# An attention and two mixtures of experts: a written order for engines through expert 0's second unit to expert 6

## The chip, the cores and the metric

One NeuronCore of a Trainium2 chip runs the whole kernel. The metric is the device time of one execution in microseconds (us), the median of several runs. Engines are named as in the profile: PE (matrix product; PEld is its weight load), DVE (vector), ACT (scalar), POOL (GpSimd), and SP, whose queue issues most DMAs.

## What is computed

Three stages follow each other, each on the output of the one before. N = 1536 tokens, width D = 512, E = 8 experts, inner width F = 1024.

```python
x = chunked_attention(q, k, v, mem_k, mem_v)      # reshaped to (1536, 512)

logits = x @ w_gate                               # first mixture: dense
P = exp(logits - logits.max())
for _ in range(8):                                # the gates are balanced
    P /= P.sum(1) + 1e-9
    P /= P.sum(0) + 1e-9; P *= N / E
out = sum(P[:, e] * (relu(x @ w1[e]) @ w2[e]) for e in range(8))

e_i = argmax(out @ w_gate2)                       # second mixture: top 1
y_i = softmax_weight_i * (relu(out_i @ w1b[e_i]) @ w2b[e_i])
```

All arithmetic is to fp32 accuracy. Each fp32 matrix is held as two fp32r parts, high and low, and each product is made of three: high by high, high by low, low by high.

## The kernel before, in words

**First mixture, direct units.** Expert 0 is done in two units (halves of F, `u` = 0 and 1). A unit takes the tokens in groups; for each group `m1_h` (L393) makes four tiles of the hidden layer, and `m1_y` (L409) one output tile per 128 tokens. In unit 1 the groups have 512 tokens, so 3 groups of 4 + 4 tiles: 24 tiles, each of 12 matmuls with 512 columns. After an `m1_h` tile ACT makes the high part of the hidden layer with a ReLU (L405), and DVE the low part (L406); after an `m1_y` tile DVE adds PSUM into `acc` (L423). There are two PSUM buffers for either kind of tile (tags `ph` and `py`).

**Experts 1 to 6** use a Strassen-like scheme with seven products in place of eight (`m1_g`, L464). For each quarter `fi` of the inner width and each half `n` of the tokens, `m1_g` makes seven products of 6 matmuls with 384 columns into four PSUM tiles A, B, C, D, and forms four hidden blocks from sums of them in the SBUF scratch `stmp` (`s1`, `s5`, `w`, `c21`). `put` (L488) lets ACT make the ReLU (L492) and DVE the low part (L493) of each block. `m1_d` (L517) then makes six output tiles of 6 matmuls with 512 columns; each is added into `acc` by DVE (L530). These six tiles lag one step: `flush_d` (L903) issues, after the products of a step, the output tiles of the step before. Output tiles use the tags `ph` and `py` in turn, so a tile can start when the fourth tile before it has been taken out of PSUM.

**What the sums need.** The scheme works on sums of blocks of x. `xs_build` (L430) makes them while unit 1 runs: `three` has POOL form three sums with eight additions and subtractions of 384 columns in `stmp`, ACT make their high part (L449) and DVE the low part (L450) in `tsum`; `one` overwrites a part of `xhi` and `xlo` that had been saved to `xkeep` in DRAM. The weights need sums too: `conv_pair` (L151) takes two raw chunks, and makes seven high and low pairs, ACT the high part (L157), POOL the low one (L158) and four sums between them (L164 to L170). Other chunks are converted one at a time by `chunk_conv` (L131; L145 on ACT, L146 on POOL). After a conversion `chunk_dma` (L119) issues the next load on SP's queue; there are four raw buffers.

**Gates.** `sinkhorn_start` and eight `sinkhorn_iter` (L359, L372) balance the gates; each iteration has four DVE operations on rows, one small matmul with a matrix of ones (`cs`), and five DVE operations on columns. `scale_expert0` (L387) then multiplies the 12 tiles of `acc` by their gates on ACT.

**What sets the order.** Outside of the last stage the order on each engine is chosen by the framework's scheduler: it takes what is written as a priority and fills engines with what it believes to be ready. What it has chosen is fixed in the program: each engine runs its own queue strictly in that order, and an instruction whose input is late holds up all that stand behind it. Within `tc.manual_schedule()` (used before for the jobs of the second mixture) the instructions keep the written order.

Of the kernel before, what the change touches and what calls it, by code (L numbers as in the profile page):

```python
# [9 lines left out]
F32 = mybir.dt.float32  # L10
# [10 lines left out]
P = 128  # L21
# [11 lines left out]
def kernel(  # L33
# [97 lines left out]
    def chunk_conv(eng=None, defer=False):  # L131
# [3 lines left out]
        if kind == "s":  # L135
            rest = conv_pair(e, u)
            if defer:
                return rest
            rest()
            return  # L140
# [10 lines left out]
    def conv_pair(e, fi):  # L151
# [9 lines left out]
        split("a11", a11)  # L161
        split("a12", a12)
        split("a22", a22)
        nc.gpsimd.tensor_tensor(a22, a21, a22, ALU.add)  # L164
        split("s1", a22)
        nc.gpsimd.tensor_tensor(a21, a11, a21, ALU.subtract)
        nc.gpsimd.tensor_tensor(a11, a22, a11, ALU.subtract)
        split("s2", a11)
        split("s3", a21)
        nc.gpsimd.tensor_tensor(a12, a12, a11, ALU.subtract)  # L170

        def rest():
            split("s4", a12)
            done[0] += 2
            chunk_dma(2)

        return rest
# [181 lines left out]
    def sinkhorn_start():  # L359
        m = smallp.tile([P, 1], F32, tag="gm", name="gm")  # L360
        nc.vector.tensor_reduce(out=m, in_=lsb, axis=AX.XY, op=ALU.max)
        mt = ps_a.tile([P, P], F32, tag="pa", name="mt")
        nc.tensor.transpose(mt[0:1, :], m, ident)
        m1 = smallp.tile([1, 1], F32, tag="m1", name="m1")
        nc.vector.tensor_reduce(out=m1, in_=mt[0:1, :], axis=AX.X, op=ALU.max)
        mb = ps_a.tile([P, 1], F32, tag="pa", name="mb")
        nc.tensor.matmul(mb, ones[0:1, :], m1, start=True, stop=True)
        nm = smallp.tile([P, 1], F32, tag="nm", name="nm")
        nc.vector.tensor_scalar_mul(nm, mb, -1.0)
        nc.scalar.activation(pr, lsb, AF.Exp, bias=nm)  # L370

    def sinkhorn_iter():  # L372
        rs = smallp.tile([P, NT, 1], F32, tag="rs", name="rs")
        nc.vector.tensor_reduce(out=rs, in_=pr, axis=AX.X, op=ALU.add)
        nc.vector.tensor_scalar_add(rs, rs, EPS)
        nc.vector.reciprocal(rs, rs)
        nc.vector.tensor_tensor(pr, pr, rs.to_broadcast([P, NT, E]), ALU.mult)
        cs = ps_a.tile([P, NT, E], F32, tag="pa", name="cs")
        nc.tensor.matmul(cs.rearrange("p t e -> p (t e)"), ones, pr.rearrange("p t e -> p (t e)"), start=True, stop=True)
        ct = smallp.tile([P, 1, E], F32, tag="ct", name="ct")  # L380
        nc.vector.tensor_reduce(out=ct.rearrange("p a e -> p e a"), in_=cs.rearrange("p t e -> p e t"), axis=AX.X, op=ALU.add)
        nc.vector.tensor_scalar_add(ct, ct, EPS)
        nc.vector.reciprocal(ct, ct)
        nc.vector.tensor_scalar_mul(ct, ct, float(N) / E)
        nc.vector.tensor_tensor(pr, pr, ct.to_broadcast([P, NT, E]), ALU.mult)
# [44 lines left out]
    def xs_build():  # L430

        steps = []
# [6 lines left out]
        def three(kk, n):  # L439
# [8 lines left out]
            for i, x in ((0, x22), (1, x12), (2, x21)):  # L448
                nc.scalar.copy(tsum[:, i, 0, kk, c], x)  # L449
                nc.vector.tensor_tensor(tsum[:, i, 1, kk, c], x, f32(tsum[:, i, 0, kk, c]), ALU.subtract)  # L450
# [13 lines left out]
    def m1_g(e, fi, n):  # L464
# [23 lines left out]
        def put(key, x):  # L488
# [658 lines left out]
```

## Time and profile before

| | us |
|---|---|
| median of 3 runs (1366.89 to 1368.7) | 1367.07 |
| the profiled execution | 1369.2 |
| span of its trace | 1367.4 |
| PE busy | 1301.5 (95%) |
| DVE busy | 728.5 (53%) |
| POOL busy | 451.2 (33%) |
| ACT busy | 435.2 (32%) |

The span runs from the first to the last traced instruction, and the profiled execution's own time is 1.8 us longer. Busy time of PE is that of modelled, overlapping matmuls, so gaps between them and the granted clock say more than the share. In time the span divides so: attention with unit 0 up to some 177 us, unit 1 to 255, experts 1 to 6 to some 1016, expert 7 and the routing to some 1185, and the second mixture from there.

### The profile page before, as it was taken

The numbers are of one execution on the slowest core, as the hardware profiler recorded it, in microseconds if no ns is written. First come the engines' busy times: TensorE is split into PE (matmuls) and PEld (weight loads), VectorE is DVE, ScalarE is ACT, GpSimd is POOL, SyncE is SP. The second block draws the span as 40 slices with busy tenths as digits, with TensorE's granted clock in tenths as the row PEclk, the third lists the DMA queues.
The fourth block names the chain that finished last, engine by engine and source line by source line (L and its number), as shares of the span: only waits on it lengthen the run. The fifth ranks groups of instructions, "written<-read, shape, count | busy, mean of one in ns | idle before, by whom it ended". The sixth has DMA issues, their size and how long they took to land. (4 is left out here: it accounts for less than half of the span.)

```text
span 1367.4 us, 18950 instructions
## 1 busy us (share of the span) xinstructions
PE 1301.5 (95%) x6892; PEld 1128.5 (83%) x6892; DVE 728.5 (53%) x1429; ACT 435.2 (32%) x927; POOL 451.2 (33%) x557
## 2 busy tenths in 40 slices
PE   8999679999999999999999999999999999989997
PEld 7888558888888888888888888888898888768775
DVE  6666456355555545555555555555653234745566
ACT  4333221523222222232223222222221122444455
POOL 4221870643333333433334444444220012301001
PEclk9999889999999999999999999999999999999999
DMA  9443540111111111111111111111120001476560
GB/s 194 92 93 86 178 164 14 54 32 39 39 32 31 31 31 32 32 31 32 31 31 31 40 38 32 32 31 38 47 93 16 1 8 45 154 235 233 158 204 16
DMA packets 107259, 94.12 MB, mean 69 GB/s; under 512 B 50667, under 2 KB 75243, under 8 KB 107140
## 3 DMA queue, kind: packets, MB, share of 16 engines
q1 hardware_dynamic: 104996, 87.30, 22.0%
q0 software_dynamic: 2000, 5.34, 1.0%
q8 instruction: 58, 0.95, 0.3%
q14 instruction: 61, 0.50, 0.1%
q10 hardware_dynamic: 144, 0.03, 0.0%
HBM read 76.27 MB, written 17.60 MB: 69 GB/s over the span
## 5 line engine op out<-in xcount | busy, mean ns | idle before, releaser
L182 PE MATMUL py<-bh,hbig 128*128 128x512 f32 x960 | 328.0, 394 | 12.4 <-ACT hbig L405 11.9
L182 PE MATMUL ph<-bh,hbig 128*128 128x512 f32 x576 | 204.3, 395 | 21.3 <-DVE acc L530 21.3
L182 PEld LDWEIGHTS py<-bh,hbig 128*128 128x128 f32 x960 | 180.8, 189 | 51.1 <-ACT hbig L405 12.6
L182 PE MATMUL py<-bl,hbig 128*128 128x512 f32 x480 | 188.4, 392 | 0.0
L182 PEld LDWEIGHTS ph<-bh,hbig 128*128 128x128 f32 x576 | 108.1, 188 | 51.3 <-DVE acc L530 30.6
L146 POOL TENSOR_TENSOR bl<-raw,bh 128x512 fp32r<-128x512 f32 x62 | 80.0, 1308 | 201.8 <-ACT bh L145 194.2
L508 POOL TENSOR_TENSOR stmp<-stmp 128x384 f32<-128x384 f32 x48 | 55.8, 1163 | 272.5 <-DVE stmp L506 272.4
L158 POOL TENSOR_TENSOR ws<-raw,ws 128x256 fp32r<-128x256 f32 x168 | 123.0, 746 | 52.0 <-ACT ws L157 50.7
L530 DVE SCALAR_TENSOR_TENSOR acc<-py,pr,acc 128x512 f32<-128x512 f32 x144 | 107.6, 748 | 42.1 <-PE py L182 42.0
L493 DVE SCALAR_TENSOR_TENSOR hbig<-stmp,hbig 128x384 fp32r<-128x384 f32 x144 | 83.0, 619 | 74.7 <-ACT hbig L492 74.7
L486 PE MATMUL sb<-tsum,ws 128*128 128x384 f32 x576 | 117.5, 340 | 0.0
L530 DVE SCALAR_TENSOR_TENSOR acc<-ph,pr,acc 128x512 f32<-128x512 f32 x144 | 107.6, 747 | 17.2 <-PE ph L182 16.4
L486 PE MATMUL sa<-xhi,ws 128*128 128x384 f32 x384 | 114.2, 338 | 0.0
L486 PE MATMUL sc<-xhi,ws 128*128 128x384 f32 x384 | 113.4, 336 | 0.6 <-ACT stmp L501 0.6
L182 PE MATMUL ph<-bl,hbig 128*128 128x512 f32 x288 | 112.9, 392 | 0.0
L493 DVE SCALAR_TENSOR_TENSOR hbig<-sa,hbig 128x384 fp32r<-128x384 f32 x48 | 26.8, 558 | 160.4 <-ACT hbig L492 160.4
L182 PEld LDWEIGHTS py<-bl,hbig 128*128 128x128 f32 x480 | 90.6, 189 | 18.9
L486 PEld LDWEIGHTS sb<-tsum,ws 128*128 128x128 f32 x576 | 103.0, 188 | 0.0
L492 ACT ACTIVATE hbig<-stmp 128x384 fp32r<-128x384 f32 x144 | 67.6, 518 | 97.9 <-POOL stmp L508 97.9
L157 ACT CAST ws<-raw 128x256 fp32r<-128x256 f32 x168 | 65.9, 408 | 90.9 <-POOL raw L164 40.8
L182 PE MATMUL ph<-xhi,ah 128*128 128x512 f32 (+1 forms) x240 | 86.9, 363 | 8.0 <-DVE hbig L406 8.0
L694 DVE TENSOR_TENSOR w<-raw,w 128x512 fp32r<-128x512 f32 x112 | 72.2, 686 | 39.9 <-ACT w L693 39.9
(210 smaller groups left out, 2264.1 us busy)
## 6 DMA issues: line engine op xcount, KB each, us to landing
raw<-in_moe_w_dram SPq DMA_DIRECT2D x176, 256.0 KB
raw<-in_moe_w_dram SPq DMA_DIRECT2D x96, 128.0 KB
disp<-zrow SPq DMA_DIRECT2D x24, 257.0 KB
xg<-disp SPq DMA_DIRECT2D x19, 257.0 KB
vin<-in_v_dram SPq DMA_DIRECT2D x20, 176.0 KB
kin<-in_k_dram SPq DMA_DIRECT2D x12, 256.0 KB
qin<-in_q_dram SPq DMA_DIRECT2D x12, 256.0 KB
out_dram<-zrow SPq DMA_DIRECT2D x12, 256.0 KB
```

The source lines that it names most:

```text
L146: (eng or nc.gpsimd).tensor_tensor(lo, raw, f32(hi), ALU.subtract)
L157: nc.scalar.copy(w[:, 0], x)
L158: nc.gpsimd.tensor_tensor(w[:, 1], x, f32(w[:, 0]), ALU.subtract)
L182: nc.tensor.matmul(ps, l, r, start=(i == 0), stop=(i == n - 1))
L486: nc.tensor.matmul(ps, l, r, start=(i == 0 and not more), stop=(i == len(terms) - 1), skip_group_check=more)
L492: nc.scalar.activation(hh, x, AF.Relu)
L493: nc.vector.scalar_tensor_tensor(hl, x, 0.0, f32(hh), ALU.max, ALU.subtract)
L508: nc.gpsimd.tensor_tensor(s5, w, s5, ALU.add)
L530: nc.vector.scalar_tensor_tensor(a, ps, pr[:, t, e:e + 1], a, ALU.mult, ALU.add)
L694: nc.vector.tensor_tensor(l, raw, f32(h), ALU.subtract)
```

## The change

The scheduler gives way to the written order from unit 1 of expert 0 to the end of expert 6, and the written order itself is new.

- **Unit 1** (`unit_sums`): a table `beside` lists for each of the 24 tiles (called steps 0 to 23 here) what is issued right behind it: the conversion of single chunks at steps 0, 1, 2 and 21; the gate work, cut into three starting parts and eight pairs of a row part and a column part, one part a step from 0 to 18; POOL's part of the four `three` at steps 3, 7, 13, 18, and their ACT and DVE parts (`three_split`) at 6 and 7, 12 and 13, 17 and 18, 22 and 23; the parts of `one` on POOL at 9 and 20, those on DVE and ACT at 12, 13, 22, 23; and the eight parts of the first weight pair at 10 to 12, 14 to 16 and 20. `stmp` grows from four to seven pieces.
- **Experts 1 to 6** (`expert_sums`): the conversion of a weight pair is cut into eight parts (`pair_steps`), two of which are issued at each of two places inside `m1_g`, over both halves of the tokens; the two single chunks are converted behind the second half. In `m1_g` the sum `s5` moves from POOL to DVE, and the low parts of three blocks are issued behind all the sums.
- `scale_expert0` moves from the end of unit 1 into the first quarter of expert 1. The rows of zeros that are written to DRAM (`fills`) are issued one a step; their preparation and the constants of the routing stand at the start of expert 1.

```diff
@@ -158,23 +154,27 @@
-        split("a11", a11)
-        split("a12", a12)
-        split("a22", a22)
-        nc.gpsimd.tensor_tensor(a22, a21, a22, ALU.add)
-        split("s1", a22)
-        nc.gpsimd.tensor_tensor(a21, a11, a21, ALU.subtract)
-        nc.gpsimd.tensor_tensor(a11, a22, a11, ALU.subtract)
-        split("s2", a11)
-        split("s3", a21)
-        nc.gpsimd.tensor_tensor(a12, a12, a11, ALU.subtract)
-
-        def rest():
+        def sums():
+            nc.gpsimd.tensor_tensor(a22, a21, a22, ALU.add)
+            nc.gpsimd.tensor_tensor(a21, a11, a21, ALU.subtract)
+            nc.gpsimd.tensor_tensor(a11, a22, a11, ALU.subtract)
+            nc.gpsimd.tensor_tensor(a12, a12, a11, ALU.subtract)
+
+        def last():
             split("s4", a12)
-            done[0] += 2
             chunk_dma(2)
 
-        return rest
+        done[0] += 2
+        return [
+            lambda: split("a11", a11),
+            lambda: split("a12", a12),
+            lambda: split("a22", a22),
+            sums,
+            lambda: split("s2", a11),
+            lambda: split("s1", a22),
+            lambda: split("s3", a21),
+            last,
+        ]
...
@@ -445,23 +455,28 @@
...
+        def three_split(kk, n, i):
+            c = slice(n * SN, (n + 1) * SN)
+            x = stmp[:, (2, 1, 3)[i], :]
+            nc.scalar.copy(tsum[:, i, 0, kk, c], x)
+            nc.vector.tensor_tensor(tsum[:, i, 1, kk, c], x, f32(tsum[:, i, 0, kk, c]), ALU.subtract)
 
         def one(kk, n):
-            (b11, b12, _, _), _, c2 = parts(kk, n)
-            x11, x12 = stmp[:, 2 * kk, :], stmp[:, 2 * kk + 1, :]
-            nc.gpsimd.tensor_tensor(x11, b11[0], b11[1], ALU.add)
+            (b11, _, _, _), _, _ = parts(kk, n)
+            nc.gpsimd.tensor_tensor(stmp[:, 4 + kk, :], b11[0], b11[1], ALU.add)
...
@@ -490,27 +505,34 @@
...
-            nc.vector.scalar_tensor_tensor(hl, x, 0.0, f32(hh), ALU.max, ALU.subtract)
             hsum[fi, n, key] = (hh, hl)
+            return lambda: nc.vector.scalar_tensor_tensor(hl, x, 0.0, f32(hh), ALU.max, ALU.subtract)
 
         prod(A, "a11")
         nc.scalar.copy(s1, A)
+        for f in first:
+            f()
         prod(B_, "s2")
         nc.vector.tensor_tensor(s1, B_, s1, ALU.add)
         prod(C, "s1")
         nc.scalar.copy(s5, C)
+        for f in second:
+            f()
         prod(D_, "a22")
         prod(A, "a12", True)
-        put((0, 0), A)
+        put((0, 0), A)()
         prod(B_, "s3")
         nc.vector.tensor_tensor(w, B_, s1, ALU.add)
         nc.vector.tensor_tensor(c21, w, D_, ALU.subtract)
-        nc.gpsimd.tensor_tensor(s5, w, s5, ALU.add)
-        put((1, 0), c21)
+        low10 = put((1, 0), c21)
+        nc.vector.tensor_tensor(s5, w, s5, ALU.add)
+        low11 = put((1, 1), s5)
         prod(C, "s4", True)
         nc.vector.tensor_tensor(s1, C, s1, ALU.add)
-        put((0, 1), s1)
-        put((1, 1), s5)
+        low01 = put((0, 1), s1)
+        low10()
+        low11()
+        low01()
...
@@ -907,58 +929,113 @@
...
+        gates = sinkhorn_parts()
+        beside = {i: [] for i in range(24)}
+        for i in range(3):
+            beside[i].append(chunk_conv)
+        for i, f in enumerate(gates):
+            beside[i].append(f)
+        kn = [(kk, n) for n in range(NQ) for kk in range(KH)]
+        for i, a in zip((6, 12, 17, 22), kn):
+            for j in range(3):
+                beside[i + (j > 1)].append(lambda a=a, j=j: three_split(*a, j))
+        for i, a in zip((3, 7, 13, 18), kn):
+            beside[i].append(lambda a=a: three(*a))
+        pair = []
+        beside[9] += [lambda: one(0, 0), lambda: one(1, 0)]
+        beside[12].append(lambda: one_split(0, 0))
+        beside[13].append(lambda: one_split(1, 0))
+        beside[10].append(lambda: pair.extend(pair_steps()))
+        for i in (10, 11, 12):
+            beside[i].append(lambda: pair.pop(0)())
+        beside[12].append(lambda: pair.pop(0)())
+        for i in (14, 15, 16):
+            beside[i].append(lambda: pair.pop(0)())
+        beside[20].append(lambda: pair.pop(0)())
+        beside[20] += [lambda: one(0, 1), lambda: one(1, 1)]
+        beside[21].append(chunk_conv)
+        beside[22].append(lambda: one_split(0, 1))
+        beside[23].append(lambda: one_split(1, 1))
+        it = 0
+        for t0 in range(0, NT, GT)[::-1]:
+            for w in [lambda f=f: m1_h(e, u, t0, GT, f) for f in range(NF)] + [lambda i=i: m1_y(e, u, t0, i) for i in range(GT)]:
+                w()
+                for f in beside[it]:
+                    f()
+                it += 1
+
+    def expert_sums(e):
+        end = e == E - 2
+        for fi in range(NF):
+            plain = end and fi == NF - 1
+            pair = [] if plain else pair_steps()
+            for n in range(NQ):
+                first, second = [], []
+                if plain and n == 0:
+                    first, second = [chunk_conv] * 2, [chunk_conv]
+                elif not plain:
+                    first, second = (pair[:2], pair[2:4]) if n == 0 else (pair[4:6], pair[6:])
+                m1_g(e, fi, n, first, second)
+                if e == 1 and fi == 0:
+                    for t in range(n * SQ, n * SQ + SQ):
+                        scale_expert0(t)
+                        scale_expert0(t + TPB)
+                flush_d()
+                late_d.append((e, fi, n))
+                if n:
+                    conv(1 if plain else 2)
+                if fills:
+                    fills.pop(0)()
...
+                with tc.manual_schedule():
+                    nc.gpsimd.memset(zrow, 0.0)
+                    nc.gpsimd.memset(zrow[:, DM:DM + 1], BIG)
+                    routing_consts()
+                    expert_sums(e)
...
-        if nu == 1:
-            gs = gs[::-1]
-            for i, z in enumerate((xhi, xlo)):
-                nc.sync.dma_start(xkeep[:, i], f32(z[:, 0:KH, S:N]))
-            ast.close()
-            sst = ExitStack()
-            spool = sst.enter_context(tc.tile_pool(name="spool", bufs=1, side="right"))
-            tsum = spool.tile([P, 3, 2, KH, S], F32R, name="tsum")
-            stmp = spool.tile([P, 4, SN], F32, name="stmp")
-            three, one = xs_build()
-            xq = {2: three[0], 5: three[1], 8: three[2], 11: three[3], 14: one[0], 16: one[1], 18: one[2], 20: one[3]}
...
```

The gates' functions are cut at the places named above without other edits (`sinkhorn_parts`).

What the change moves is shown at three places. The first is ACT at the end of unit 0 and the start of unit 1 (`hbig` is the hidden layer, `tsum` the sums of x, `ah` and `bh` chunks of weights, `ws` parts of a pair). Before:

```order
L405 ACTIVATE hbig<-ph 128x256
L449 CAST tsum<-stmp 128x384 x6
L405 ACTIVATE hbig<-ph 128x256 x2
L449 CAST tsum<-stmp 128x384 x3
L405 ACTIVATE hbig<-ph 128x256
L145 CAST ah<-raw 128x512
L405 ACTIVATE hbig<-ph 128x256
L449 CAST tsum<-stmp 128x384 x3
L145 CAST bh<-raw 128x512
```

Now:

```order
L416 ACTIVATE hbig<-ph 128x256
L416 ACTIVATE hbig<-ph 128x512
L139 CAST bh<-raw 128x512
L416 ACTIVATE hbig<-ph 128x512
L139 CAST bh<-raw 128x512
L416 ACTIVATE hbig<-ph 128x512
L139 CAST bh<-raw 128x512
L377 ACTIVATE pr<-lsb,nm 128x96
L416 ACTIVATE hbig<-ph 128x512
L462 CAST tsum<-stmp 128x384 x3
L416 ACTIVATE hbig<-ph 128x512 x3
L153 CAST ws<-raw 128x256
```

Twelve casts of `tsum` stood among the ReLUs of unit 0's last tiles (those of 256 columns), six of them in a row. Now none stands there, and the first three come behind the four ReLUs of unit 1's first group.

The second is POOL in one quarter of an expert (`bl` the low part of a chunk, `raw` the raw buffers). Before:

```order
L508 TENSOR_TENSOR stmp<-stmp 128x384
L146 TENSOR_TENSOR bl<-raw,bh 128x512 x2
L158 TENSOR_TENSOR ws<-raw,ws 128x256 x3
L164 TENSOR_TENSOR raw<-raw 128x2x128
L166 TENSOR_TENSOR raw<-raw 128x2x128
L167 TENSOR_TENSOR raw<-raw 128x2x128
L158 TENSOR_TENSOR ws<-raw,ws 128x256
L170 TENSOR_TENSOR raw<-raw 128x2x128
L158 TENSOR_TENSOR ws<-raw,ws 128x256 x2
L508 TENSOR_TENSOR stmp<-stmp 128x384
L158 TENSOR_TENSOR ws<-raw,ws 128x256
L508 TENSOR_TENSOR stmp<-stmp 128x384
```

Now:

```order
L140 TENSOR_TENSOR bl<-raw,bh 128x512 x2
L154 TENSOR_TENSOR ws<-raw,ws 128x256 x3
L158 TENSOR_TENSOR raw<-raw 128x2x128
L159 TENSOR_TENSOR raw<-raw 128x2x128
L160 TENSOR_TENSOR raw<-raw 128x2x128
L161 TENSOR_TENSOR raw<-raw 128x2x128
L154 TENSOR_TENSOR ws<-raw,ws 128x256 x4
```

The sum `s5` in `stmp` stood once behind a whole pair's sums and once alone; now POOL has no part in the hidden blocks.

The third is DVE at steps 12 and 13 of unit 1, now:

```order
L434 TENSOR_TENSOR acc<-py,acc 128x512
L390 TENSOR_REDUCE ct<-cs 128x8
L391 TENSOR_SCALAR ct<-ct 128x8
L392 RECIPROCAL ct<-ct 128x8
L393 TENSOR_SCALAR ct<-ct 128x8
L394 TENSOR_TENSOR pr<-pr,ct 128x96
L463 TENSOR_TENSOR tsum<-stmp,tsum 128x384 x2
L472 TENSOR_TENSOR stmp<-xhi,xlo 128x384
L473 TENSOR_TENSOR stmp<-stmp 128x384
L475 TENSOR_TENSOR xlo<-stmp,xhi 128x384
L434 TENSOR_TENSOR acc<-py,acc 128x512
```

Between the two additions into `acc` stand a column part, two low parts of sums, and three operations of `one`, which in the order before were spread by the scheduler.

## Rows read from the trace of the kernel before

**Rows 1.** The waits of PE over the span: engine line waited for, us in total, times, longest.

```profile
PE ph L182 <- DVE acc L530: 21.3, 22, 1.5
PE py L182 <- ACT hbig L405: 11.9, 2, 9.8
PE ph L182 <- DVE hbig L406: 8.0, 3, 6.3
```

**Rows 2.** The timeline of PE: start us, us, engine line op out<-in xcount [idle before <-releaser].

```profile
151.21 0.28 PE L182 MATMUL ph<-xlo,ah 128*128 128x256 f32 x1
151.33 0.28 PE L182 MATMUL ph<-xhi,al 128*128 128x256 f32 x1
...
161.44 0.80 PE L182 MATMUL py<-bh,hbig 128*128 128x512 f32 x1 [9.83 <-ACT hbig L405]
...
176.93 0.39 PE L182 MATMUL ph<-xhi,ah 128*128 128x512 f32 x1
...
254.87 0.33 PE L486 MATMUL sa<-xhi,ws 128*128 128x384 f32 x1
```

**Rows 3.** The timeline of ACT in the same stretch.

```profile
158.25 0.51 ACT L449 CAST tsum<-stmp 128x384 fp32r<-128x384 f32 x1 [6.26 <-POOL stmp L445]
```

**Rows 4.** Windows: PE, PEld, DVE, ACT, POOL busy us (xcount); then PEclk, DMA share, GB/s.

```profile
160.00:180.00 20.00, 15.60 (x62) 12.43 (x63) 8.59 (x11) 5.09 (x12) 19.53 (x19) 0.77 0.09 32
220.00:240.00 20.00, 20.00 (x94) 16.61 (x93) 14.24 (x46) 3.34 (x6) 0.00 (x0) 1.00 0.00 1
```

**Rows 5.** The timeline of PE in a slice of expert 2.

```profile
498.10 0.39 PE L182 MATMUL ph<-bh,hbig 128*128 128x512 f32 x1
...
503.35 0.39 PE L182 MATMUL py<-bh,hbig 128*128 128x512 f32 x1
504.68 0.50 PE L182 MATMUL ph<-bh,hbig 128*128 128x512 f32 x1 [0.94 <-DVE acc L530]
```

**Rows 6.** The timelines of POOL, ACT and DVE in that slice; last row the next.

```profile
501.01 1.33 POOL L508 TENSOR_TENSOR stmp<-stmp 128x384 f32<-128x384 f32 x1
...
502.37 0.94 ACT L492 ACTIVATE hbig<-stmp 128x384 fp32r<-128x384 f32 x2 [1.84 <-POOL stmp L508]
...
503.88 0.74 DVE L530 SCALAR_TENSOR_TENSOR acc<-ph,pr,acc 128x512 f32<-128x512 f32 x1
...
517.81 0.75 DVE L530 SCALAR_TENSOR_TENSOR acc<-ph,pr,acc 128x512 f32<-128x512 f32 x1
```

**Rows 7.** The timeline of DVE in the second unit, POOL idle.

```profile
200.68 0.25 DVE L374 TENSOR_REDUCE rs<-pr 128x12 f32<-128x96 f32 x1
201.44 0.26 DVE L377 TENSOR_TENSOR pr<-pr,rs 128x96 f32<-128x96 f32 x1
201.63 0.69 DVE L423 TENSOR_TENSOR acc<-py,acc 128x512 f32<-128x512 f32 x1
...
204.34 0.69 DVE L423 TENSOR_TENSOR acc<-py,acc 128x512 f32<-128x512 f32 x1 [2.03 <-PE py L182]
204.95 0.25 DVE L381 TENSOR_REDUCE ct<-cs 128x8 f32<-128x96 f32 x1
...
205.88 0.26 DVE L385 TENSOR_TENSOR pr<-pr,ct 128x96 f32<-128x96 f32 x1
...
220.57 0.56 DVE L456 TENSOR_TENSOR stmp<-xhi,xlo 128x384 f32<-128x384 f32 x1
```

**Rows 8.** The timeline of DVE in the second unit, POOL at work.

```profile
181.84 2.31 DVE L456 TENSOR_TENSOR stmp<-xhi,xlo 128x384 f32<-128x384 f32 x2
184.07 2.61 DVE L457 TENSOR_TENSOR stmp<-stmp 128x384 f32<-128x384 f32 x2
```

**Rows 9.** The timeline of ACT at the end of the second unit.

```profile
242.54 1.96 ACT L388 ACTIVATE acc<-acc,pr 128x512 f32<-128x512 f32 x3
```

**Rows 10.** The timeline of SP's queue, then a window of 3 us, in expert 3.

```profile
525.93 8.77 SPq L125 DMA_DIRECT2D raw<-in_moe_w_dram  x4
...
539.00:542.00 3.00, 3.00 (x18) 2.79 (x17) 1.44 (x3) 0.48 (x1) 0.00 (x0) 1.00 0.00 0
```

More of the change, by code (lines that the diff above doesn't have):

```diff
@@ L149, in chunk_conv, with pair_steps @@
         chunk_dma()
-    def conv_pair(e, fi):
+    def pair_steps():
+        e, fi = chunks[done[0]][:2]
         r0, r1 = raw_view(raws.pop(done[0])), raw_view(raws.pop(done[0] + 1))
@@ L357 @@
     nc.vector.memset(ones, 1.0)
[L359 to L370, printed above, removed]
@@ L459, in one, with m1_g @@
             nc.vector.tensor_tensor(xlo[:, kk, c2], x12, f32(xhi[:, kk, c2]), ALU.subtract)
-        kn = [(kk, n) for n in range(NQ) for kk in range(KH)]
-        return [lambda a=a: three(*a) for a in kn], [lambda a=a: one(*a) for a in kn]
-    def m1_g(e, fi, n):
+        return three, three_split, one, one_split
+    def m1_g(e, fi, n, first, second):
         c = slice(n * SN, (n + 1) * SN)
@@ L908, in flush_d, with unit_sums @@
                     m1_d(e_, fi_, n_, half, i)
+    def unit_sums(e, u):
+        nonlocal spool, tsum, stmp
+        spool = sst.enter_context(tc.tile_pool(name="spool", bufs=1, side="right"))
+        tsum = spool.tile([P, 3, 2, KH, S], F32R, name="tsum")
+        stmp = spool.tile([P, 7, SN], F32, name="stmp")
+        three, three_split, one, one_split = xs_build()
+        gates = sinkhorn_parts()
[32 more added lines that the diff above has]
+                it += 1
@@ L910 @@
+    spool = tsum = stmp = None
+    sst = ExitStack()
     for nu, (e, u) in enumerate(units):
         last = nu == len(units) - 1
+        if nu == 1:
+            for i, z in enumerate((xhi, xlo)):
+                nc.sync.dma_start(xkeep[:, i], f32(z[:, 0:KH, S:N]))
+            ast.close()
+            with tc.manual_schedule():
+                unit_sums(e, u)
+            psst.close()
+            continue
         if 0 < e < E - 1:
@@ L918 @@
                 zrow = zst.enter_context(tc.tile_pool(name="zp", bufs=1, side="right")).tile([P, ROW], F32, name="zrow")
[L919 to L920 removed]
                 fills = fill_list(zrow)
                 conv(1)
[L923 to L930 removed]
+                with tc.manual_schedule():
+                    nc.gpsimd.memset(zrow, 0.0)
+                    nc.gpsimd.memset(zrow[:, DM:DM + 1], BIG)
+                    routing_consts()
+                    expert_sums(e)
@@ L958 @@
         L = sum(NF + nt for _, nt in gs)
-        convs = ([13, 15, 16, 25] if nu == 0 else [21] if nu == 1 else [4, 7, 10, 14])
-        if nu != 1:
-            convs += [L - 3]
+        convs = ([13, 15, 16, 25] if nu == 0 else [4, 7, 10, 14]) + [L - 3]
         if nu:
@@ L1033 @@
             flush()
-        if nu == 0:
-            post = [sinkhorn_start] + [sinkhorn_iter] * 8
-        if nu == 1:
-            for p_ in post:
-                p_()
-            post = []
-            for t in range(NT):
-                scale_expert0(t)
-            psst.close()
-            routing_consts()
     for f in first_load:
```

105 lines of the change are left out of this document (48 added, 57 removed).

## The prediction

> **What bounds the kernel now.** I read the waits of PE first, since PE has work in nearly every microsecond and nothing else is near full. Over the whole span its three largest waits add up to 41 us [rows 1], and the timelines put all of them between unit 0's end and expert 6, where the change works. They are of two kinds.
>
> *Unit 0's tail and unit 1.* PE's timeline shows the last matmul of a run at 151.33 us, then nothing for 9.83 us; unit 1 starts at 176.93 and expert 1's first product at 254.87 [rows 2]. The reader is to see who ended that pause: a ReLU on ACT. ACT at that time ran a cast of `tsum` at 158.25 after waiting 6.26 us for POOL [rows 3]. The ReLU stood behind that cast in ACT's queue, PE behind the ReLU. In the order before, twelve such casts stand among unit 0's last ReLUs. The windows show the second half of the bill: from 160 to 180 us the granted clock of PE averaged 0.77, between its two levels of 1.2 and 2.4 GHz, and at 220 to 240, after unbroken work, 1.00 [rows 4].
>
> How much is lost there? At 151.4 us unit 0 still had 24 matmuls of 256 columns, at 0.12 us from one to the next [rows 2], and 24 of 512 columns. A tile of 12 of those takes 2.71 us, from one of its two additions into `acc` to the next [rows 7], so 0.226 each. That is 2.9 + 5.4 = 8.3 us. Unit 1 is 24 tiles of 2.71 us, 65.0, and some ten tiny gate matmuls, for which I allow 1.4 together. Needed: 74.7. Taken: 254.87 - 151.45 = 103.4. **28.7 us are lost.**
>
> *Experts 1 to 6.* PE waits 22 times for DVE to take an output tile out of PSUM, 21.3 us [rows 1], with 48 steps in the stage. In one of them the output tiles start at 498.10; the fifth, which needs the first one's buffer, starts at 504.68, 1.33 us after the last matmul before it where 0.23 is normal [rows 5]. So one such wait costs 1.10 us. The chain behind it: POOL makes `s5` at 501.01 behind a whole weight pair's conversion, ACT's ReLU waits 1.84 us for that, DVE's low part waits for the ReLU, and only at 503.88 does DVE take the first tile out, 5.8 us after it was begun [rows 6]. Other steps have no such wait. **22 x 1.10 = 24.2 us.**
>
> **The change part by part.** *1. `s5` on DVE, the pair spread.* POOL leaves the hidden blocks' chain. DVE gains a sum of 384 columns, 0.56 us without POOL beside it [rows 7]. Behind the last product DVE then has at most `s5`, one more sum, three low parts: 5 x 0.56 = 2.8, some 3.1 with the latency. The fifth tile is due 4 x 1.36 = 5.4 us after the first begins, and taking one out lasts 0.74 [rows 6], so DVE may be as late as 4.7. If POOL runs beside all five, each costs 1.16 to 1.31 [rows 8], 6.2 in sum, and 1.5 us of wait come back. I take the low end with one slowed operation, 3.8: a pair's parts are issued behind the first and third of seven products, so POOL is through with them near the last. Term: **-24.2**, bounds -24.2 and +9 (1.5 x 22 in their place).
>
> *2. Casts of `tsum` out of unit 0's ReLUs.* The 28.7 us go, except what is new. POOL keeps the same additions, now beside unit 1; the single chunks' and the pair's conversion move inside unit 1, too. Unit 0's tail keeps its normal change from hidden to output tiles; I leave 1 us for it (0.5 to 2).
>
> *3. DVE in unit 1: the new wait.* The gate's small matmul is issued right behind each tile and waits for the row part of the tile before, and PE's queue stands behind it. At most steps DVE has one addition (0.69) or low part and a row part, 1.02, or column part, 1.19 [rows 7]: under 2.0 of 2.71 us. Steps 12 and 13 are not like that. Step 12 has 0.69 + 1.19, five operations on two SBUF inputs, and a trip to ACT between the last two (0.6); step 13 has 0.69 + 1.02, then four more and a trip. Such an operation lasts 0.56 with POOL idle [rows 7], 1.16 to 1.31 with POOL at work [rows 8].
> With POOL idle: step 12 takes 5.3, step 13's row part ends 0.3 + 5.3 + 1.7 = 7.3 us after the tile of step 12, where PE, two tiles on, wants it after 5.4: 1.9 lost. The rest of step 13 (2.8) and steps 14 and 15 (1.9 + 1.7) end at 13.7, PE wants the next at 4 x 2.71 + 1.9 = 12.7: 1.0 lost. Sum 2.9.
> With POOL at work: step 12 takes 8.5, the row part ends at 10.5, 5.1 lost; then 10.5 + 5.4 + 3.6 = 19.5 against 15.9, 3.6 lost; and steps 22 and 23 with nine such operations run some 4.5 us into expert 1's first step. Sum 13.2. The two longer pauses may also drop the clock to the lower level: the mean of 0.77 over the 20 us that held the pause at 161 and a shorter one is worth 0.23 x 20 = 4.6 us at most [rows 4]. That makes 18.
> At step 12 ACT is itself held by this step's casts, so POOL has little to do; later it is at work. I take 2 + 3.5 for the two waits, 1.5 for the four steps with a low part and a row part in one, 1.5 for the end: **+8.5**, bounds 3 and 18.
>
> Here a rule bears on the sum. The Trainium skill, SBUF — State Buffer, section Who interferes with whom, says that DVE with two SBUF inputs and GpSimd share a port pair as an exclusive lock and that the loser blocks for the whole instruction. The rows agree in kind (0.56 becomes 1.16 to 1.31). By that rule, held throughout, the sum would go to this part's upper bound, which is case (a) below.
>
> *4. Gates on `acc`, 12 multiplications on ACT in expert 1.* Three take 1.96 us [rows 9], six 3.9. They stand behind the first step's ReLUs, and ahead of the second step's copy of product A, which is over 4.2 us (four products of 6 x 0.175) into that step wanted empty; there are no output tiles yet between. The multiplications end some 1.4 + 3.9 us after the first step's products, the copy 0.5 later: **+2** (0 to 4).
>
> *5. Loads and zeros on SP's queue.* The pair's four loads now are issued behind its last part, about 12 us before the next pair's first cast. In the trace four issues went out by 534.7 us, and from 539 no byte moved [rows 10]: 4.3 us at the most. Cover is 12 us, and if it were gone ACT would wait with the ReLUs behind. The zeros go out one a step. 0.
>
> **The sum**: -24.2 - 28.7 + 1 + 8.5 + 2 = -41.4, less than 0.6 either way for the wait in expert 1's first step that is in neither term. Small waits that a fixed order always has somewhere I put at 2: **-39.4**. The profiled execution took 1369.2, so 1329.8; it stands 2.1 above the median of the runs, so **1328 us** in their terms.
>
> **The rivals.**
> (a) *DVE beside POOL is the bound of unit 1*, each of its two-input operations at 1.2 us: +18 and +4 in place of +8.5 and +2, so 1328 + 11.5 = 1340. For it: every such row beside POOL is doubled [rows 7, 8]. Against it: POOL waits for DVE and ACT in turn. Chance 0.15. The page of the Trainium skill on SBUF named above would have it so.
> (b) *DVE is never late in unit 1*: +3 and 0, no 2 us for small waits: 1328 - 9.5 = 1318. For it: the operations spread over POOL's own pauses. Chance 0.12.
> (c) *The wait in experts 1 to 6 stays*, as `s5` on DVE delays the first tile as POOL did: 1328 + 24 = 1352. For it: five operations beside POOL reach 6.2 of 4.7 us. Against: the spread pair. Chance 0.06.
> (d) *Slower*: the pair's loads come late. Each load waits for the last part of the pair before it, the first cast stands in ACT's queue ahead of `s5`'s copy and all ReLUs, and PE needs the copy within 3 us. If landing takes over 12 + 3 us, each further microsecond costs one in 22 quarters; from 1.8 us beyond, 16.8 in all, the gain is gone; with 3 us it is 1328 + 66 = 1394. Against it: 4.3 us at the most in the trace. Chance 0.03.
> (e) *The order stays as it was in effect*, because instructions are still moved across the blocks: the preparation of the zeros was. The order shows ReLUs and casts as written. 1367. Chance 0.02.
>
> **How the numbers follow.** The forecast has 0.62. The range takes its own bounds, and most of (a) and (b): 1317 to 1344. 0.2% is 2.7 us, about what a measurement of this kernel can tell from no change. Faster: the forecast, (a), (b) and (c), 0.95; same 0.02; slower 0.03.
>
> **What would show it.** In the new profile PE's wait for ACT's `hbig` of some 10 us is gone, and the granted clock stays at 1.00 from 140 to 240 us apart from two dips at most; expert 1's first product starts near 237. The 22 waits for DVE's `acc` are gone, and successive quarters of an expert start 31.3 us apart in place of 32.4. PE waits for DVE at the gate matmuls (`cs`) behind steps 14 and 16, 5 us or so. POOL's sum `s5` no longer stands in its list. Wrong it would be if waits of PE for ACT or for a load of `raw` appear in every quarter, or if unit 1 takes more than 90 us.

## The result and the profile after

The changed kernel takes 1325.05 us (1320.35 to 1326.91) where the kernel before takes 1367.21: a ratio of 0.9684, 95% interval 0.9658 to 0.9711, 42 us less. The forecast was 1328 (1317 to 1344). The profiled execution took 1324.86, its span 1322.8.

The waits of PE in the changed kernel (L501 is a product of experts 1 to 6, L388 the gate matmul, L512 ACT's copy of product A):

```profile
PE cs L388 <- DVE pr L384: 5.9, 4, 2.8
PE sa L501 <- ACT stmp L512: 2.1, 1, 2.1
PE sb L501 <- DVE stmp L516: 0.8, 1, 0.8
```

The three waits of [rows 1], 41 us, are gone, the one that came 22 times too. PE's timeline gives the milestones to set beside [rows 2]: the start of unit 1, the two longest gate waits, expert 1's first product, and the wait for ACT in its second step.

```profile
160.09 0.39 PE L182 MATMUL ph<-xhi,ah 128*128 128x512 f32 x1
...
206.85 0.43 PE L388 MATMUL cs<-pr,ones 128*128 128x96 f32 x2 [1.75 <-DVE pr L384]
...
215.61 0.43 PE L388 MATMUL cs<-pr,ones 128*128 128x96 f32 x2 [2.83 <-DVE pr L384]
...
236.85 0.33 PE L501 MATMUL sa<-xhi,ws 128*128 128x384 f32 x1
...
251.84 0.44 PE L501 MATMUL sa<-xhi,ws 128*128 128x384 f32 x1 [2.09 <-ACT stmp L512]
```

Unit 1 begins 16.8 us earlier (176.93 before) and takes 76.8 us where it took 77.9; expert 1's first product is 18.0 earlier. From there to the last product of expert 6 the time fell from 760.8 to 735.1 us, 25.7 less. A quarter of an expert is two steps; the distance from one step's first product to the next step's was 15.59 and 16.85 in turn (21 long ones), and is 15.59 in all 45 now; only the first two steps of expert 1, which have no output tiles between them, grew together from 25.61 to 26.47. 21 x 1.26 = 26.5, less 0.9, makes up the 25.7 but for rounding. After expert 6 nothing changed by more than 0.9 us. One long distance of the kernel before, and the same one now:

```profile
490.71 0.33 PE L486 MATMUL sa<-xhi,ws 128*128 128x384 f32 x1
...
507.55 0.33 PE L486 MATMUL sa<-xhi,ws 128*128 128x384 f32 x1
```

```profile
481.52 0.33 PE L501 MATMUL sa<-xhi,ws 128*128 128x384 f32 x1
...
497.11 0.33 PE L501 MATMUL sa<-xhi,ws 128*128 128x384 f32 x1
```

The windows over the former pause and over the new dip, to set beside [rows 4]:

```profile
160.00:180.00 20.00, 19.36 (x87) 15.40 (x86) 9.20 (x21) 5.73 (x11) 12.55 (x12) 1.00 0.13 40
...
200.00:220.00 20.00, 15.42 (x62) 12.05 (x61) 16.31 (x37) 3.26 (x8) 15.27 (x17) 0.92 0.00 1
```

The granted clock, 0.77 in 160 to 180 us before, is 1.00, and between 140 and 240 it is below that in one window only, 0.92, where the two longer waits lie.

So the sum came true in both halves. Whether for the reasons given is another matter, and most runs went to that: each undoes or adds one thing, and is read by its time, by the distance between steps, and by PE's waits. Behind each time stands, in brackets, its ratio to the kernel before with the 95% interval; "more" is against the 1325 of the changed kernel.

### The profile page after: what moved, and what is told of

Same layout as the page of the kernel before. It is cut to its first block, busy times and chain, and to the rows that moved or that the text cites. A ratio compares the mean times of both kernels' runs of the same rounds, so it can differ in the third digit from the quotient of the medians.

```text
span 1322.8 us, 18917 instructions
## 1 busy us (share of the span) xinstructions
PE 1290.9 (98%) x6892; PEld 1127.2 (85%) x6892; DVE 756.5 (57%) x1477; ACT 428.0 (32%) x927; POOL 400.9 (30%) x509
## 5 line engine op out<-in xcount | busy, mean ns | idle before, releaser
L182 PE MATMUL ph<-bh,hbig 128*128 128x512 f32 x576 | 201.5, 390 | 0.0
L512 ACT COPY stmp<-sa 128x384 f32<-128x384 f32 x48 | 23.1, 480 | 314.5 <-PE sa L501 314.5
L501 PE MATMUL sb<-tsum,ws 128*128 128x384 f32 x576 | 117.6, 340 | 0.8 <-DVE stmp L516 0.8
L501 PE MATMUL sa<-xhi,ws 128*128 128x384 f32 x384 | 114.4, 338 | 2.1 <-ACT stmp L512 2.1
L501 PE MATMUL sc<-xhi,ws 128*128 128x384 f32 x384 | 113.3, 335 | 0.0
L501 PEld LDWEIGHTS sb<-tsum,ws 128*128 128x128 f32 x576 | 103.0, 188 | 1.1 <-DVE stmp L516 1.1
L507 ACT ACTIVATE hbig<-stmp 128x384 fp32r<-128x384 f32 x144 | 71.4, 525 | 93.5 <-DVE stmp L526 83.9
L182 PE MATMUL ph<-xlo,ah 128*128 128x512 f32 (+1 forms) x240 | 84.1, 351 | 0.0
L182 PE MATMUL ph<-xhi,al 128*128 128x512 f32 (+1 forms) x240 | 84.1, 351 | 0.0
```

The costliest lines, as they stand in the source:

```text
L182: nc.tensor.matmul(ps, l, r, start=(i == 0), stop=(i == n - 1))
L501: nc.tensor.matmul(ps, l, r, start=(i == 0 and not more), stop=(i == len(terms) - 1), skip_group_check=more)
L507: nc.scalar.activation(hh, x, AF.Relu)
```

## Experiments

### Experts 1 to 6: which part ends the 22 waits?

**s5 back on POOL** (e1).

```diff
-        nc.vector.tensor_tensor(s5, w, s5, ALU.add)
+        nc.gpsimd.tensor_tensor(s5, w, s5, ALU.add)
```

> The changed kernel with the sum s5 put back on POOL, the pair's eight parts still spread over two steps. Theory A, spreading the pair is what ends the 22 waits (POOL has no long run of work ahead of s5 any more): within 3 us of the changed kernel's 1325, quarters still 31.2 us apart. Rival B, s5's engine is what ends them: waits of PE for DVE at acc come back in most of the 23 quarters, 1.27 us each, so 24 to 29 us more, 1349 to 1354.

1328.49 us (0.971, 0.9694 to 0.9727), 3.4 more. All 45 distances are still 15.59; the first two steps took 30.17 in place of 26.47, and that is the whole loss. Theory A allowed 3 and fits by the distances, so far.

**The pair in one piece** (e2).

```diff
-                    first, second = (pair[:2], pair[2:4]) if n == 0 else (pair[4:6], pair[6:])
+                    pass
                 m1_g(e, fi, n, first, second)
+                if n == 0:
+                    for f in pair:
+                        f()
```

> The changed kernel with all eight parts of a pair issued together behind a quarter's first step, s5 left on DVE. Theory A, the spread is what counts: the casts of the last parts wait for POOL in ACT's queue ahead of the second step's copy of product A, and PE waits for ACT or DVE once a quarter, 1 to 3 us, so 23 to 70 us more than 1325. Rival B, s5's engine counts and the place of the pair does not: within 3 us of 1325, quarters 31.2 us apart.

1332.13 us (0.9747, 0.9726 to 0.9767), 7 more, but the distances are again 15.59 throughout; the first two steps took 33.93. Neither part by itself, then.

**Both undone** (e3): the two edits together.

> The changed kernel with both undone: s5 on POOL and the pair in one piece behind a quarter's first step, all in written order. Theory, these two together are the gain in experts 1 to 6: 26 to 29 us more than 1325, quarters near 32.4 us apart as in the kernel before. Rival, the written order by itself is the gain: within 5 us of 1325.

1332.92 us (0.974, 0.9724 to 0.9757), 8 more, and every distance after the first two steps, 34.11, is 15.59. With `s5` on POOL and the pair in one piece, as before, the 22 waits stay away. The rival is right in substance: the written order ends them without these two edits, which are worth 8 us together, in the first two steps of expert 1 only. ACT's casts still wait for POOL in every quarter, up to 4.2 us, but behind the ReLUs of one step and early for the next: the copy of product A, next in ACT's queue, still waits for PE.

```profile
472.57 0.41 ACT L153 CAST ws<-raw 128x256 fp32r<-128x256 f32 x1 [4.21 <-POOL raw L160]
...
475.06 0.48 ACT L512 COPY stmp<-sa 128x384 f32<-128x384 f32 x1 [0.65 <-PE sa L501]
```

**Experts 1 to 6 given back to the scheduler** (e4): `s5` on DVE and the pair in eight parts stay as written.

```diff
-            with tc.manual_schedule():
+            with ExitStack():
                 expert_sums(e)
```

> The changed kernel with experts 1 to 6 given back to the scheduler, which then chooses the order on each engine; s5 on DVE and the pair's parts written as in the change; unit 1 stays in written order. Theory, what is written and on which engine it stands is the gain, the fixed order only keeps it: within 5 us of 1325. Rival, the fixed order itself is needed: waits of PE of 1 us or more in most quarters, 1345 or more.

1347.01 us (0.9842, 0.9823 to 0.9862), 22 more. PE's wait for DVE at `acc` is back 22 times, with every second distance 16.26 to 16.31: 21 x 0.70 = 14.7 us. Another 7.2 are in the first two steps (33.67), which the kernel before did in 25.61; there PE waits for a copy of product A:

```profile
247.61 0.69 PE L501 MATMUL sa<-xhi,ws 128*128 128x384 f32 x1 [5.93 <-ACT stmp L512]
```

ACT's timeline of one of the long steps (L153 is a cast of the pair, L160 one of POOL's sums of it, L507 a ReLU) tells what the scheduler did:

```profile
481.18 0.48 ACT L518 COPY stmp<-sc 128x384 f32<-128x384 f32 x1 [0.64 <-PE sc L501]
481.56 0.41 ACT L153 CAST ws<-raw 128x256 fp32r<-128x256 f32 x1
485.26 0.41 ACT L153 CAST ws<-raw 128x256 fp32r<-128x256 f32 x1 [3.29 <-POOL raw L160]
485.57 0.48 ACT L507 ACTIVATE hbig<-sa 128x384 fp32r<-128x384 f32 x1
486.07 1.02 ACT L153 CAST ws<-raw 128x256 fp32r<-128x256 f32 x3
487.73 0.53 ACT L507 ACTIVATE hbig<-stmp 128x384 fp32r<-128x384 f32 x1 [0.63 <-DVE stmp L526]
```

The cast at 485.26 waits 3.29 us for POOL, and the ReLU of product A stands behind it. It was written for the next step; the scheduler had put it ahead of this one's ReLUs. The kernel before, where the pair was written behind the ReLUs, had been given the same order, and its ACT timeline, in the slice of [rows 6], says so:

```profile
494.08 0.48 ACT L501 COPY stmp<-sc 128x384 f32<-128x384 f32 x1 [0.64 <-PE sc L486]
494.46 0.41 ACT L157 CAST ws<-raw 128x256 fp32r<-128x256 f32 x1
496.54 0.41 ACT L157 CAST ws<-raw 128x256 fp32r<-128x256 f32 x1 [1.67 <-POOL raw L164]
496.86 0.49 ACT L492 ACTIVATE hbig<-sa 128x384 fp32r<-128x384 f32 x1
```

The new theory: casts that wait for POOL stand in ACT's queue ahead of ReLUs that are due; `s5` behind the pair on POOL is a second cause beside it. Four runs test it.

**One cast moved** (e9), in written order.

```diff
-                    first, second = (pair[:2], pair[2:4]) if n == 0 else (pair[4:6], pair[6:])
+                    first, second = (pair[:2], pair[2:5]) if n == 0 else (pair[5:6], pair[6:])
```

> The changed kernel, all in written order, with one thing moved: the cast of the weight sum s2, which needs POOL's sums of the pair, goes from the second step's first place to the first step's second place, so that on ACT it stands ahead of that step's ReLUs. Theory, a cast that waits for POOL ahead of the ReLUs is what made PE wait once a quarter wherever the scheduler set the order: the ReLU of product A comes 2.3 us later, PE waits once a quarter as in the run with experts 1 to 6 given to the scheduler, quarters 31.9 us apart in place of 31.2, so 23 x 0.7 = 16 us more than 1325, about 1341. Rival, DVE's five operations or the engine of s5 decide: within 3 us of 1325.

1331.17 us (0.9733, 0.9716 to 0.9749), 6 more, of which some 2.7 are in the first two steps (29.18). The ReLU's delay is as foretold, 6.53 us behind the copy of A in place of 4.21 in the other step of the quarter, in which no cast stands ahead:

```profile
483.31 0.48 ACT L512 COPY stmp<-sa 128x384 f32<-128x384 f32 x1 [6.63 <-PE sa L501]
...
489.52 0.41 ACT L153 CAST ws<-raw 128x256 fp32r<-128x256 f32 x1 [3.32 <-POOL raw L160]
489.84 0.48 ACT L507 ACTIVATE hbig<-sa 128x384 fp32r<-128x384 f32 x1
```

But a quarter loses 0.26 us (distances of 15.83 and 15.87), not 0.7. In e4 DVE's chain from the low part of A to the last low part lasted 4.42 us (486.08 to 490.50), here 3.95 (490.36 to 494.31): there the other three casts come early too, POOL makes their low parts beside DVE, and `s5` on DVE lasts 0.93 in place of 0.55. So one cast was sized too dear; the kind is confirmed by the control. That the other three casts make up the rest of e4's 0.70 is read from these rows; no run adds them alone.

**The control** (e10): a fourth cast in the same place that waits for nothing.

```diff
-            lambda: split("a22", a22),
+            lambda: (split("a22", a22), nc.scalar.copy(wts[e, fi, "a11"][:, 0], a11)),
```

> The control to the run before: in the same place ahead of the first step's ReLUs a fourth cast that waits for nothing (a11 is cast a second time to the same place). Theory, the wait for POOL counts and not ACT's time: quarters stay 31.2 us apart, within 3 us of 1325. Rival, ACT's time for one more cast ahead of the ReLUs is what makes them late: some 16 us more, as in the run before.

1323.58 us (0.9675, 0.9659 to 0.9691): no change. ACT's timeline has the added cast (L171) and no wait ahead of the ReLU but that for the product:

```profile
481.85 0.41 ACT L153 CAST ws<-raw 128x256 fp32r<-128x256 f32 x1
482.16 0.41 ACT L171 CAST ws<-raw 128x256 fp32r<-128x256 f32 x1
483.58 0.49 ACT L507 ACTIVATE hbig<-sa 128x384 fp32r<-128x384 f32 x1 [1.01 <-PE sa L501]
```

ACT's time costs nothing there; its wait does.

**The scheduler's order by hand** (e11), with `s5` on POOL.

```diff
-        put((0, 0), A)()
+        low00 = put((0, 0), A)
+        for f in third:
+            f()
+        low00()
...
-        nc.vector.tensor_tensor(s5, w, s5, ALU.add)
+        nc.gpsimd.tensor_tensor(s5, w, s5, ALU.add)
...
-                    first, second = (pair[:2], pair[2:4]) if n == 0 else (pair[4:6], pair[6:])
-                m1_g(e, fi, n, first, second)
+                    first, second, third = (pair[:2], pair[2:5], pair[5:]) if n == 0 else ([], [], [])
+                m1_g(e, fi, n, first, second, third)
```

> The order that the scheduler had chosen in the kernel before, written out by hand on ACT and DVE in experts 1 to 6: two casts behind the copy of A, two behind the copy of C, three between the ReLU of A and the other three ReLUs, and s5 on POOL behind the whole pair. Theory, the order is all there was: PE's wait for DVE at acc is back in every quarter, quarters 32.4 to 33.2 us apart (s5 stands behind one split more than it did before), so 28 to 46 us more than 1325 with the first step's 4 us. Rival, the scheduler cost something besides the order: under 10 us more.

1371.05 us (1.003, 1.002 to 1.004): 46 more, and no better than the kernel before. PE's list of waits begins

```profile
PE ph L182 <- DVE acc L555: 35.3, 22, 1.6
```

with every second distance 17.50 or 17.53, so a quarter loses 1.9 us where the kernel before lost 1.26. An order written out by hand gives back all of the loss, and more: it is the order, not who sets it. From e3 this run differs only in where the pair's parts are written, among the step's copies and ReLUs or behind them all; that is worth some 38 us.

**The kernel before with s5 on DVE** (e12), and nothing else.

> The kernel before with one thing changed: s5 is added on DVE in place of POOL; the scheduler still sets the order. Theory, of the 1.27 us that a quarter lost, 0.7 came from the casts ahead of the ReLUs and stay, and some 0.56 came from s5 on POOL and go: 22 x 0.56 = 12 us less than the kernel before, 1355, quarters 31.9 us apart. Rival, s5 on POOL was the cause of the whole wait, as the prediction had it: 28 us less, 1339, quarters 31.2 us apart.

1353.43 us (0.9894, 0.9877 to 0.991), 14 less than the kernel before (1367.46 beside it); distances of 16.19 to 16.22. Of the 1.26 us a quarter lost, `s5` on POOL made 0.65, and 0.61 stays. The casts stand where they stood and still wait for POOL in every quarter, up to 2.4 us at L164. PE's waits in this run, to set beside [rows 1]: the one in unit 0 is as it was, the other comes as often and is a third as long.

```profile
PE py L182 <- ACT hbig L405: 11.9, 2, 9.9
PE ph L182 <- DVE acc L530: 7.6, 22, 0.9
```

### Unit 0's end and unit 1

**Unit 1 given back to the scheduler** (e5).

```diff
-            with tc.manual_schedule():
+            with ExitStack():
                 unit_sums(e, u)
```

> The changed kernel with the second unit of expert 0 given back to the scheduler; experts 1 to 6 stay in written order. The casts of tsum then stand among unit 0's last ReLUs on ACT again. Theory, that place is what cost 18 us in the kernel before: PE waits some 10 us for a ReLU near 150 us, the clock falls, and expert 1's first product comes near 255 in place of 237: 1343 (1338 to 1350). Rival, the gain of 18 us came from the gate's parts being spread and the work being moved to other steps, not from the order: within 5 us of 1325.

1344.67 us (0.9838, 0.9821 to 0.9856), 20 more; unit 1 begins at 176.16 and expert 1's first product comes at 256.7. The casts of `tsum` (L462) are among unit 0's ReLUs (L416) again, as in [rows 3], and wait for POOL. ACT, then PE:

```profile
159.12 0.51 ACT L462 CAST tsum<-stmp 128x384 fp32r<-128x384 f32 x1 [5.50 <-POOL stmp L455]
160.19 0.51 ACT L462 CAST tsum<-stmp 128x384 fp32r<-128x384 f32 x1 [0.56 <-POOL stmp L456]
161.46 0.51 ACT L462 CAST tsum<-stmp 128x384 fp32r<-128x384 f32 x1 [0.75 <-POOL stmp L457]
161.88 0.65 ACT L416 ACTIVATE hbig<-ph 128x256 fp32r<-128x256 f32 x2
```

```profile
163.50 0.58 PE L182 MATMUL ph<-xhi,ah 128*128 128x256 f32 x1 [14.03 <-DVE hbig L417]
```

The theory holds; that it is the place of these casts, and not something else in the scheduler's order, is read from these rows, as no run moves the casts alone. That the 20 us of this run and the 22 of e4 add up to the 42 of the result is in part chance: 7 of e4's 22 lie in two steps in which the kernel before was not slower, and some 12 of what that kernel lost in experts 1 to 6 do not come back in e4, where `s5` stays on DVE.

**POOL's sums left out** (e6).

```diff
-            beside[i].append(lambda a=a: three(*a))
+            if i == 3:
+                beside[i].append(lambda: nc.gpsimd.memset(stmp[:, 0:4, :], 0.0))
```

> POOL's 32 sums of x for tsum are left out (a zeroing of stmp stands in for them, so the products with tsum are not the reference's); DVE and ACT do all that they did. Theory, DVE is late in unit 1 because POOL's sums run beside it: the gate's small operations are all under 0.4 us, the four waits of PE at the gate matmuls shrink from 5.9 to 3 us or less, and the time falls by 3 to 5 us, to about 1321. Rival, DVE is late because steps 12 and 13 hold too many of its own operations: the waits stay within 1 us of 5.9, the time within 1.5 us of 1325.

1358.68 us, but that is no measure: the second mixture is routed by the data, and the time behind expert 6 rose from 350.9 to 391.5. Unit 1 can be read: 72.4 us in place of 76.8 (it began at 160.2 here and 160.1 there), and the gate waits are 3.6 us in place of 5.9, neither under 3 nor within 1 of 5.9. DVE's groups of 160 to 237 us (line engine op names shapes xcount | busy us, mean ns) in the changed kernel, then in this run:

```profile
L384 DVE TENSOR_TENSOR pr<-pr,rs 128x96 f32<-128x96 f32 x8 | 4.3, 542 | 0.3
...
L393 DVE TENSOR_SCALAR ct<-ct 128x8 f32<-128x8 f32 x8 | 3.5, 438 | 0.3
...
L390 DVE TENSOR_REDUCE ct<-cs 128x8 f32<-128x96 f32 x8 | 2.0, 249 | 0.0
```

```profile
L384 DVE TENSOR_TENSOR pr<-pr,rs 128x96 f32<-128x96 f32 x8 | 2.4, 299 | 0.3
...
L390 DVE TENSOR_REDUCE ct<-cs 128x8 f32<-128x96 f32 x8 | 2.0, 250 | 0.0
...
L393 DVE TENSOR_SCALAR ct<-ct 128x8 f32<-128x8 f32 x8 | 1.4, 172 | 0.3
```

The gate's small operations are lengthened by POOL's work beside them, some of them; that makes up to 4.4 us of unit 1. The wait behind step 14 stays, at 1.76; the one behind step 16 is 1.29 in place of 2.83. It is 1.24 to 1.27, though, in four runs with all of POOL's sums (e2, e9, e10 and e11), so POOL's share in it is not settled.

**One block's sums later** (e7).

```diff
-        beside[12].append(lambda: one_split(0, 0))
-        beside[13].append(lambda: one_split(1, 0))
...
+        beside[18].append(lambda: one_split(0, 0))
+        beside[19].append(lambda: one_split(1, 0))
```

> The changed kernel with the first two of the four sums and splits that DVE makes of a single block of x moved from steps 12 and 13 of unit 1 to steps 18 and 19. Theory, they are what makes DVE late for the gate matmuls behind steps 14 and 16: those two waits, 1.75 and 2.83 us, go, a new one of up to 1 us may stand at steps 19 and 20 where no gate matmul follows; expert 1's first product comes 3.5 to 4.5 us earlier, 1321. Rival, the lateness has its cause elsewhere in the steps (the pair's parts on POOL and ACT): the waits stay, 1325.

1320.44 us (1320.04 to 1323.57; 0.9664, 0.9645 to 0.9684), unit 1 in 73.8 us from a start at 158.0; with a start near that it took 75.2 in four other runs that leave unit 1 as changed, e2, e9, e10 and e11. Like for like that is 1.4 us, less than the 3.5 to 4.5 foretold. The waits of PE from 130 to 260 us:

```profile
PE sa L501 <- ACT stmp L512: 2.1, 1, 2.1
PE cs L388 <- DVE pr L384: 2.0, 3, 0.7
PE py L182 <- ACT hbig L416: 1.0, 1, 1.0
PE py L182 <- DVE acc L434: 0.6, 1, 0.6
```

The wait of 2.83 is gone, and 0.62 is left of that of 1.75. The new waits, 1.0 and 0.6 at steps 20 and 22, are a little over what was allowed for. The theories of both of the last two runs are right in part: DVE was late because steps 12 and 13 hold much, and POOL beside it lengthens what they hold.

**The gate multiplications spread as well** (e8).

```diff
+                if e == 1 and fi == 0 and n:
+                    first, second = list(first), list(second)
+                    for t in range(SQ):
+                        first.append(lambda t=t: scale_expert0(t))
+                        second.append(lambda t=t: scale_expert0(t + TPB))
                 m1_g(e, fi, n, first, second)
-                if e == 1 and fi == 0:
-                    for t in range(n * SQ, n * SQ + SQ):
+                if e == 1 and fi == 0 and n:
+                    for t in range(SQ, 2 * SQ):
```

> As the run before, and the first six gate multiplications of acc in expert 1 taken out of the queue between the first step's ReLUs and the second step's copy of product A: three behind the pair's first two casts of the second step, three behind its last two. Theory, the 2.1 us wait of PE for that copy goes and nothing new comes: 2 us below the run before, 1319 (5.5 to 6.5 below the changed kernel). Rival, the multiplications hold ACT's copy of product C or the ReLUs of the second step instead: 1321 or more.

1320.44 us (1317.53 to 1321.77; 0.965, 0.9631 to 0.9668). The 2.1 us wait is gone from the trace, new ones of 0.4 for ACT's copy of C and 0.7 for DVE at `acc` stand there, and the first two steps take 25.01 us where e7 has 26.83. By the traces these 1.8 us last to the end of expert 6 (733.6 us from expert 1's first product, 735.4 in e7); the median, the same as in e7, does not show them, so the forecast of 2 us less was missed. These two are the fastest versions found, 4.6 below the changed kernel's median; the intervals of their ratios overlap with its own, so for this gain the traces are the better evidence: in e8 unit 1 took 73.8 us from a start at 160.3, where the changed kernel took 76.8.

## Why the prediction was right, and where its reasons were not

*What bounds the kernel*: right in place and in size. The two stages named hold all of the gain but 0.9 us. By the traces 44.6 us went, 5 more than the 39.4 forecast; by the medians 42, since the profiled execution before stood 2 above its median and that of the changed kernel did not. These 5 us are, in the main, term 1, whose wait was taken as 1.10 us and cost 1.26 (21 x 0.16 = 3.4), and the 2 for small waits, which did not come.

*Term 1, -24.2 for `s5` on DVE and the spread pair*: the size was right (21 x 1.26 = 26.5; one wait had been taken as 1.10), the reason was not. The chain was followed back from DVE to the ReLU and from there to `s5` on POOL [rows 6], and there it ended, with a cause found. Five rows earlier in ACT's list stood a second one, a cast that waits 1.67 us for POOL ahead of the ReLU of A. e12 shows that `s5` alone would have been worth 14 us; e4, that with `s5` moved and the pair cut, but the order left to the scheduler, 22 us are missing; e3, that the written order needs neither of the two. What ends the waits is that in written order no cast is still waiting for POOL's sums when the ReLUs behind it are due: in the changed kernel none waits for them in experts 2 to 6, and in e3 they wait between one step's ReLUs and the next step's copy. That the sum came out near was luck as to the cause: any of the routes ends at a DVE that is in time, and once it is, more earliness is worth nothing. The concern over DVE's five operations beside POOL, the upper bound of +9, did not come up: most lasted 0.56.

*Term 2, -28.7, and 1 for unit 0's tail*: right, and nothing for the tail: its last 48 matmuls run from 151.75 to 160.09, 8.3 us, without a wait. e5 bears out the cause as named.

*Term 3, +8.5 for a late DVE*: unit 1 took 76.8 us where 66.4 were counted as needed, so 10.4. Place and kind were right, steps 14 and 16 with 1.75 and 2.83 (2 and 3.5 foretold); two smaller waits make 1.35. Right behind the longest the granted clock was 0.50, the lower level, from 216.8 to 220.0 us; that is the 0.92 of its window, and makes 1.6. Together 7.5. The other 2.9 are no wait: the last four tiles, with no gate work behind them, begin 2.72 us apart, and the tiles from the second on to the twentieth take 3.9 us in all beyond that, their waits and the clock, where 1.4 was allowed for the gate's small matmuls between them. In e6, where the clock did not fall, this is 3.5. So that allowance was the term mis-sized. At the unit's end 0.8 came of 1.5.

Here the rule on the shared port was weighed. The Trainium skill, SBUF — State Buffer, section Who interferes with whom, has `tensor_tensor` with two SBUF inputs contend with GpSimd's reads, lets `tensor_scalar` do so in some modes, and on this chip `tensor_reduce` never. The groups above agree line by line: the reduction stays at 249 and 250 ns with and without POOL's sums (it reads PSUM; L381, a reduction that reads SBUF, stays at 241 and 243), the other two go from 299 and 172 to 542 and 438. That rule held throughout would have made case (a), 1340; it was not the bound, since POOL has pauses: in one of 5.7 us DVE did nearly all of step 12's five operations, which took 0.56 at most.

*Term 4, +2 for the gate multiplications*: 2.09 measured, at the copy foretold.

*Small waits, +2*: none showed in experts 1 to 6.

*The rivals*: (a) and (b) were outside on either side, as 10.4 lies between 3 and 18. (c), that the wait stays, and (e), that the order stays, did not occur. (d), late loads, is nowhere: no wait of PE for `raw`, and none for ACT but the 2.09 us of term 4.

## What to carry to other kernels

When a wait is followed back to a queue, read the whole queue ahead of the late instruction, not only the instruction that released it: two causes in a row show the later one alone, and taking that away uncovers the other. A conversion of weights that needs a second engine between its own steps belongs behind the work that the matmuls wait for; a cast in the same place costs nothing when it waits for nothing, and a wait as long costs nothing behind the ReLUs (e10, e3). And a part of a change that looks decisive should be undone by itself: here two parts of the change to experts 1 to 6 could go back at 8 us, while the order could not, at 22 us there and 20 in unit 1.

## What was not expected of the hardware

Very small DVE operations are stretched by POOL far beyond their own length. The multiplication of 8 values in each partition (L393), 0.17 us alone, took up to 0.81 in unit 1, an addition to 8 values (L391) and a product of 96 (L394) up to 1.01:

```profile
189.16 0.81 DVE L393 TENSOR_SCALAR ct<-ct 128x8 f32<-128x8 f32 x1
...
212.41 1.01 DVE L394 TENSOR_TENSOR pr<-pr,ct 128x96 f32<-128x96 f32 x1
...
224.78 1.01 DVE L391 TENSOR_SCALAR ct<-ct 128x8 f32<-128x8 f32 x1
```

POOL's operations on 384 columns last 1.0 to 1.3 us, and the stretched operation waits for the rest of one of them. The first of the three rows ends at 189.97, and this operation of POOL's at 189.94:

```profile
188.93 1.01 POOL L455 TENSOR_TENSOR stmp<-stmp 128x384 f32<-128x384 f32 x1
```

So it goes in all of the changed kernel's unit 1: the 12 `TENSOR_SCALAR` of the gate that began while an operation of POOL's had more than 0.17 us to run ended 0.03 us after it, the 7 `TENSOR_TENSOR` 0.11 us after it, and the others took 0.17 and 0.26 us. The reductions and the reciprocals (L383, L392) kept their length beside POOL. In e6 most of the stretching goes when POOL's sums go.

Unit 1 began either at 157.6 to 158.3 us or at 160.1 to 160.3 in the profiled executions in which it was in written order, though unit 0 is the same in all of them, and the second of the two longer gate waits was 1.24 or 2.83 with it. Between the changed kernel and e10, 1.7 us of it is already there 24 us into the span, in the attention. This would spread single executions of the changed kernel by some 3.6 us at expert 1's first product (236.85 here, 233.21 in e10), and is why e1, e2, e3, e9 and e10 are read by the distances between steps more than by their medians.
